# One operation order for every step becomes two tables; weight pairs and expert choice move with it

## The chip, the cores and the metric

The program runs on one core of one Trainium2 chip, in one launch. The metric is device time in microseconds (us) of that core. The engines are TensorE (PE), VectorE (DVE), ScalarE (ACT), GpSimd (POOL) and SyncE (SP, which issues most DMAs here). Each executes its own queue in order, and they wait for each other by semaphores.

## What is computed

Three layers follow each other: attention in which each row keeps its 32 largest scores, a gated dense layer, and a layer in which each token goes to one of eight experts.

```python
def _attn_ref(q, k, v):                     # 4 batches, 8 heads, 576 tokens, 64 wide
    scores = scale * np.matmul(q, k.transpose(0, 1, 3, 2))
    kth = np.partition(scores, -top_k, axis=-1)[..., -top_k:-top_k + 1]
    scores = np.where(scores >= kth, scores, -1000000000.0)
    scores = scores - np.max(scores, axis=-1, keepdims=True)
    attn = np.exp(scores)
    attn = attn / (np.sum(attn, axis=-1, keepdims=True) + 1e-09)
    return np.matmul(attn, v)
def _moe_ref(x, w_in, w_out):               # 2304 tokens, 512 wide, 2048 inside
    h = x @ w_in
    g = h * np.clip(h + 3.0, 0.0, 6.0) / 6.0
    return g @ w_out
def _moe2_ref(x, expert_emb, tau, w1, w2):  # 8 experts, 512 to 1024 to 512
    logits = normalized(x) @ normalized(expert_emb).T / tau
    expert_idx = np.argmax(logits, axis=1)
    ...
        h = np.maximum(x[mask] @ w1[e], 0.0)
        out[mask] = gate_w[mask, None] * (h @ w2[e])
```

The weights `w_in` and `w_out` arrive as 64-bit floats.

## The kernel before

Matrix products are made of parts: an operand x is held as a high part in a format that TensorE takes and a low part x - high, and a product is three matmuls (high·high, high·low, low·high).

**Units and steps.** The attention is cut into 72 units. A unit is 128 query rows of two heads (kind "t"), or the last 64 rows of four heads (kind "r"). The loop has 76 steps. Step i makes the scores of unit i (`scores`, `take`, `pairs`), searches the 32 largest of unit i-1 (`select`, four rounds), masks unit i-2 (`relu`, `mask`), takes the exponent and scales unit i-3 (`expo`, `guard`, `inverse`, `scale`), and turns unit i-4 and multiplies it by V (`turned`, `keep`, `values`, `finish`). Inside this loop nothing is reordered by a scheduler (`tc.manual_schedule`): on each engine the instructions stand as `step` calls them. `scale` runs on ACT for the first 16 units and on POOL afterwards.

**The dense layer** is mixed in. When 256 tokens have their attention, `push_group` queues eight items; one item is taken per step, but not in the eight steps of `PAUSE`. The item's first product `s1` (24 matmuls of 256 columns) fills one PSUM bank, `gate` on ACT and `swish` on DVE read it, `large` on ACT and `small` on POOL make the two parts, and the second product `s2` (12 matmuls of 512 columns) follows a step later. The low parts of the weights lie in DRAM and are fetched again for each group (`fetch`, one item ahead). The first item is taken in step 12; 16 items remain for after the loop.

**The weights** go through 32 pairs of pieces before they can be used. `load_w` issues loads into five staging buffers, `convert_w` turns a pair from 64 to 32 bits (DVE at L221, L223 and, for one piece in four, L229; for the other three ACT at L226 and POOL at L227), and `split_w` makes the high part (ACT) and the low part (POOL, L241) and stores the low part (SP, L236) when it is next called. `words` calls `convert_w` once per step for i < 8 and twice afterwards, so the pairs end in step 19. We call the stretch up to there the ramp.

**Expert choice.** When a group's output leaves PSUM, `route` queues four operations (`r1`, `r2`, `r4`, `r5`) for each of its two blocks of 128 tokens; a step takes one. They make the logits, their argmax (DVE L606 to L609), the token's place in its expert's list (PE, POOL, DVE L619 to L627), and write it to a table in DRAM by an indirect DMA on POOL. After 16 of 18 blocks `order` sorts the experts by load; after the loop a scheduler places the rest of the dense layer, the routing and the expert stage.

The lines that set the order in a step before:

```python
        part(a, 1)                 # s1, then gate, swish
        part(a, 2)
        part(a, 3)
        words()
        for c in range(2):
            at_(4, turned, c)
            at_(4, keep, c)
        at_(0, scores, 0)
```

Of the kernel before, what the change touches and what calls it, by code (L numbers as in the profile page):

```python
# [20 lines left out]
DM, FF = 512, 2048  # L21
# [17 lines left out]
PAUSE = (13, 17, 31, 35, 49, 53, 66, 67)  # L39
HS = S // 2  # L40
# [4 lines left out]
SIDE = 100  # L45
# [38 lines left out]
def layers(tc: tile.TileContext, qt, kt, v, w_in, w_out, embt, tau, w1, w2, out, y_dram, g_dram, x_dram, tbl, lo_dram, flag, pools, consts):  # L84
# [13 lines left out]
    acc = const.tile([128, E], BF16, name="acc")  # L98
# [3 lines left out]
    viol = const.tile([128, NUNIT, 2, 2], BF16, name="viol")  # L102

# [32 lines left out]
    def embed(part):  # L136
# [6 lines left out]
        elif part == 1:  # L143
            onesf = mp.tile([128, 128], F32, tag="ug", name="onesf", bufs=4)
# [15 lines left out]
    def setup():  # L160
        nc.vector.memset(ones, 1.0)
        nc.vector.memset(acc, 0.0)
        nc.gpsimd.iota(iota8, pattern=[[1, 8]], base=0, channel_multiplier=0, allow_small_or_imprecise_dtypes=True)
        nc.gpsimd.iota(ebase, pattern=[[STRIDE, 8]], base=0, channel_multiplier=0, allow_small_or_imprecise_dtypes=True)
# [5 lines left out]
        padt = mp.tile([128, E * STRIDE * 2 // 128], I32, tag="ug", name="padt", bufs=4)  # L170
        nc.gpsimd.memset(padt, PAD)
        nc.sync.dma_start(out=tbl.rearrange("(p a) b -> p (a b)", p=128), in_=padt)
        zr = mp.tile([128, DM], F32, tag="ug", name="zr", bufs=4)
# [7 lines left out]
    wpieces = deque()  # L181
# [7 lines left out]
    wraw = deque()  # L189
    whole_w, small_w = deque(), deque()  # L190
    cnt = [0]

    def load_w():

        while wpieces and len(wraw) < 5:
            src, dst = wpieces.popleft()
            if src.dtype == F32:
# [5 lines left out]
            wraw.append((raw, dst, src.dtype == F32))  # L203

    def convert_w():


        load_w()
        words, two = [], [wraw.popleft() for _ in range(min(2, len(wraw)))]
        if not two:  # L210
            return
        both = mp.tile([128, DM], F32, tag="ug", name="wf", bufs=4)
        for o, (raw, dst, single) in enumerate(two):
            full = both[:, 256 * o:256 * o + 256]
            if single:
                nc.vector.tensor_copy(full, raw)
            else:
                cnt[0] += 1
                words.append((raw, full.bitcast(I32), cnt[0] % 4 != 3))
        for raw, t, _ in words:  # L220
            nc.vector.scalar_tensor_tensor(t, raw[:, :, 1], 3, raw[:, :, 1], op0=ALU.logical_shift_left, op1=ALU.bitwise_xor)  # L221
        for raw, t, _ in words:
            nc.vector.scalar_tensor_tensor(t, t, 0x3FFFFFFF, raw[:, :, 1], op0=ALU.bitwise_and, op1=ALU.bitwise_xor)  # L223
        for raw, t, rounded in words:
            if rounded:
                nc.scalar.activation(raw[:, :, 0], raw[:, :, 0].bitcast(U32), AF.Copy, scale=2.0 ** -29)  # L226
                nc.gpsimd.tensor_tensor(t, t, raw[:, :, 0], op=ALU.add)  # L227
            else:
                nc.vector.scalar_tensor_tensor(t, raw[:, :, 0], 29, t, op0=ALU.logical_shift_right, op1=ALU.bitwise_or)  # L229
        whole_w.append((both,) + two[0][1])  # L230

    def split_w():

        while small_w:
            lo, full = small_w.popleft()
            nc.sync.dma_start(out=lo, in_=full)  # L236
        while whole_w:
            full, hi, lo = whole_w.popleft()
            x = full if len(hi.shape) == 2 else full.rearrange("p (k n) -> p k n", k=2)
            nc.scalar.copy(hi, x)  # L240
            nc.gpsimd.tensor_tensor(x.bitcast(F32R), x, hi.bitcast(F32), op=ALU.subtract)  # L241
            small_w.append((lo, full))
# [4 lines left out]
    def fetch(n, m):  # L247

        if m < total and m not in lows_[n]:
# [224 lines left out]
    def finish(i):  # L474
# [15 lines left out]
        if p == 3:  # L490
            X = xt[b, t // 2]
            if t % 2:
                push_group(X, [4 * b + t - 1, 4 * b + t])

# [595 lines left out]
```

## Time and profile before

| | |
|---|---|
| median of 3 runs | 1183.14 us (1183.0 to 1194.14) |
| the profiled execution, its own time | 1184.85 us |
| its span, first to last instruction | 1183.1 us |
| mean granted TensorE clock | 0.938 |
| busy: PE, DVE, ACT, POOL | 1026.0, 838.1, 732.1, 645.7 us |

The span is the profiled execution without 1.75 us around it. Busy shares are means over stages with different limits, so they are read by stretch. PE's busy time includes modelled ends of matmuls that overlap: a stream of matmuls counts as busy without being at its peak. DVE is the busiest engine in the first fifth, PE from then on.

### The profile page before, as it was taken

The numbers are of one execution on the slowest core, as the hardware profiler recorded it, in microseconds if no ns is written. First come the engines' busy times: TensorE is split into PE (matmuls) and PEld (weight loads), VectorE is DVE, ScalarE is ACT, GpSimd is POOL, SyncE is SP. The second block draws the span as 40 slices with busy tenths as digits, with TensorE's granted clock in tenths as the row PEclk, the third lists the DMA queues.
The fourth block names the chain that finished last, engine by engine and source line by source line (L and its number), as shares of the span: only waits on it lengthen the run. The fifth ranks groups of instructions, "written<-read, shape, count | busy, mean of one in ns | idle before, by whom it ended". The sixth has DMA issues, their size and how long they took to land. (4 is left out here: it accounts for less than half of the span.)

```text
span 1183.1 us, 21477 instructions
## 1 busy us (share of the span) xinstructions
PE 1026.0 (87%) x7224; PEld 885.8 (75%) x7224; DVE 838.1 (71%) x2714; ACT 732.1 (62%) x1518; POOL 645.7 (55%) x846
## 2 busy tenths in 40 slices
PE   2476766699999899999899999999998898999994
PEld 1354555578888788888788878889987787888883
DVE  6999977998899998899998899611244343445440
ACT  5688768777777877777877787642334343444540
POOL 5667767686777786777786766623231433113200
PEclk9966778789999999999999998999998899999997
DMA  7335555655324445424454333346781564244540
GB/s 212 120 100 174 164 177 187 195 179 197 122 90 155 127 160 184 121 89 155 115 183 157 121 92 115 110 142 178 210 276 32 187 217 171 71 176 147 174 166 20
DMA packets 97113, 176.49 MB, mean 149 GB/s; under 512 B 21135, under 2 KB 46882, under 8 KB 96991
## 3 DMA queue, kind: packets, MB, share of 16 engines
q1 hardware_dynamic: 92351, 164.90, 43.4%
q0 software_dynamic: 4640, 10.10, 2.5%
q8 instruction: 60, 0.98, 0.3%
q14 instruction: 62, 0.51, 0.1%
HBM read 155.87 MB, written 19.71 MB: 148 GB/s over the span
## 5 line engine op out<-in xcount | busy, mean ns | idle before, releaser
L420 POOL TENSOR_TENSOR s<-s,z 128x576 f32<-128x576 f32 x144 | 186.0, 1292 | 13.0 <-ACT z L416 11.5
L530 PE MATMUL bank_h<-xh,vh 128*128 128x256 f32 x576 | 172.1, 299 | 2.7 <-ACT xh L488 1.6
L530 PE MATMUL bank_h<-xh,lo 128*128 128x256 f32 x576 | 166.7, 289 | 7.1 <-DMA lo<-lo_dram 7.1
L530 PE MATMUL bank_h<-xl,vh 128*128 128x256 f32 x576 | 166.2, 288 | 0.6 <-DVE xl L489 0.6
L399 DVE MAX8 A<-left 128x8 f32<-128x288 f32 (+1 forms) x288 | 160.0, 596 | 0.0
L453 PE MATMUL bank_t<-ident,s 128*128 128x128 f32 x648 | 110.2, 297 | 53.1 <-ACT s L440 26.1
L547 POOL TENSOR_TENSOR gl<-u,gh 128x512 fp32r<-128x512 f32 x72 | 93.2, 1294 | 79.0 <-ACT gh L544 78.0
L453 PEld LDWEIGHTS bank_t<-ident,s 128*128 128x128 f32 x648 | 76.1, 149 | 75.8 <-ACT pt L458 37.7
L368 PE MATMUL ps_sc<-kst,qh 128*128 128x288 f32 x256 | 88.8, 359 | 49.1 <-ACT s L371 24.1
L536 ACT ACTIVATE u<-bank_h,half 128x512 f32<-128x512 f32 x72 | 49.5, 687 | 118.9 <-PE bank_h L530 118.9
L563 PE MATMUL y<-wh,gh 128*128 128x512 f32 x288 | 120.0, 418 | 0.0
L530 PEld LDWEIGHTS bank_h<-xh,vh 128*128 128x128 f32 x576 | 113.3, 197 | 8.1 <-issue 3.1
L530 PEld LDWEIGHTS bank_h<-xh,lo 128*128 128x128 f32 x576 | 113.2, 196 | 8.3 <-DMA lo<-lo_dram 8.3
L563 PE MATMUL y<-lo,gh 128*128 128x512 f32 x288 | 115.9, 403 | 0.0
L530 PEld LDWEIGHTS bank_h<-xl,vh 128*128 128x128 f32 x576 | 113.4, 197 | 1.4 <-DVE xl L489 1.0
L735 DVE TENSOR_TENSOR l<-a,h 128x1024 fp32r<-128x1024 f32 x64 | 77.4, 1232 | 51.9 <-ACT h L734 45.7
L563 PE MATMUL y<-wh,gl 128*128 128x512 f32 x288 | 114.2, 401 | 0.0
L416 ACT ACTIVATE z<-s,zb 128x576 bf16<-128x576 f32 x144 | 112.7, 782 | 1.0 <-DVE zb L405 0.8
L426 ACT ACTIVATE s<-s,nb 128x576 f32<-128x576 f32 x144 | 111.7, 775 | 0.0
L458 ACT COPY pt<-bank_t 128x384 f32<-128x384 f32 x216 | 95.6, 479 | 24.4 <-PE bank_t L453 24.4
L540 DVE SCALAR_TENSOR_TENSOR u<-u,bank_h 128x512 f32<-128x512 f32 x72 | 49.2, 684 | 83.8 <-ACT u L536 83.7
L471 PE MATMUL bank_a<-pt,vt 128*64 128x128 f32 (+1 forms) x1600 | 105.4, 285 | 0.0
(230 smaller groups left out, 2819.9 us busy)
## 6 DMA issues: line engine op xcount, KB each, us to landing
lo<-lo_dram SPq DMA_DIRECT2D x144, 512.0 KB, 4.3
a<-in_moe_w_dram SPq DMA_DIRECT2D x64, 512.0 KB, 8.7
kraw<-in_k_dram SPq DMA_DIRECT2D x64, 144.0 KB, 2.6
qraw<-in_q_dram SPq DMA_DIRECT2D x64, 128.0 KB, 3.3
w<-in_moe_w_in_dram SPq DMA_DIRECT2D x32, 256.0 KB, 3.9
w<-in_moe_w_out_dram SPq DMA_DIRECT2D x32, 256.0 KB, 3.5
lo_dram<-wf SPq DMA_DIRECT2D x32, 256.0 KB, 2.1
vt<-in_v_dram SPq DMA_DIRECT2D x16, 320.0 KB, 4.1
```

Of the source, the lines that this page charges most:

```text
L368: nc.tensor.matmul(ps[:, n, :HS], t, kk[:, HS * g:HS * g + HS], start=(o == 0), stop=(o == len(parts) - 1))
L399: nc.vector.max(A[:, n, 8 * r:8 * r + 8], src[:, n, :w])
L416: nc.scalar.activation(zb_[n], tile_of(i, n), AF.Relu, bias=sel[i][2][:, n:n + 1], scale=-BIG)
L420: nc.gpsimd.tensor_tensor(s, s, zb_[n], op=ALU.subtract)
L426: nc.scalar.activation(s, s, AF.Exp, bias=sel[i][1][:, n:n + 1], scale=SCALE, accum_out=sums[i][:, n:n + 1])
L453: nc.tensor.transpose(pp[:, 128 * k:128 * k + 128], e[:, 128 * (3 * c + k):128 * (3 * c + k) + 128], ident)
L458: nc.scalar.copy(pts[i][:, 3 * c:3 * c + 3, :].rearrange("p k n -> p (k n)"), tb_.pop((i, c))[:, :384])
L471: nc.tensor.matmul(av[64 * n:64 * n + 64, c0:c1], vt[:, k, 64 * n:64 * n + 64], pt[:, k + 5 * n if k < 4 else 4, c0:c1], start=(o == 0), s ...
L530: nc.tensor.matmul(ph[:, a, :], w, x[:, k, :], start=(k == 0 and n == 0), stop=(k == 3 and n == 2))
L547: nc.gpsimd.tensor_tensor(state[q][1], state.pop((q, "u")).rearrange("p (a n) -> p a n", a=2), state[q][0].bitcast(F32), op=ALU.subtract)
L563: nc.tensor.matmul(state["y"][o], x[:, a, c], w, start=(f == 0 and n == 0), stop=(f == 15 and n == 2))
L735: nc.vector.tensor_tensor(lo, x, hi.bitcast(F32), op=ALU.subtract)
```

## The change

Five things change at once.

- **Two tables.** `step` no longer calls its parts in one written order. Some fifty small operations have names, and a step executes them as the table `FIRST` (i < 21) or `THEN` lists them. `s1` is cut into its two halves (`s10`, `s11`), `finish` into `xh` and `xl`.
- **Weight pairs in fixed phases.** Pair n belongs to step n for n < 5, and from step 5 on each step has two. The loads of a pair stand in the step before it, its conversion (`one`, `two`, `round`, `add`) in its step, high part, low part and store (`hi`, `low`, `store`) in the step after it. The pairs end in step 18.
- **Bounds.** The two DVE instructions per step that make the bias of `relu` (L405) are dropped; the POOL instruction that made the bias of `expo` now makes both, by a table `kb`.
- **Expert choice for four blocks at once.** `choose` and `rank` replace the argmax and the places of four blocks (two outside the loop); `place` writes one block's rows to the DRAM table per step.
- The side work after the loop gets a scheduler priority of 600 in place of 100, and the temporaries live in a pool of three buffers and one of one in place of four.

```diff
+RAMP, WORDS = 5, 21
+FIRST = ("turn0 lows hi0 expo0 low0 hi1 s10 keep0 load_k expo1 turn1 bend0 one0 guard pick0 store0 score0 low1 two0 mask0 pick1 "
+         "turn2 inverse s11 pick2 round1 bend1 keep1 take0 keep2 load_q mask1 s20 score1 round0 gate one1 scale two1 values swish "
...
+THEN = ("pick0 turn0 turn1 expo0 keep0 s10 expo1 lows turn2 pick1 pick2 s11 keep1 keep2 guard bend0 score0 gate take0 load_k "
+        "values mask0 score1 inverse swish scale pick3 bend1 xh load_q take1 prep need_v mask1 bounds aside large s20 xl pairs "
...
-SIDE = 100
+SIDE = 600
...
+    def pair_of(i, c):
+        n = (i if c == 0 else -1) if i < RAMP else 2 * i - RAMP + c
+        return n if 0 <= n < 32 else -1
...
+    def w_one(n):
+        e = ent_[n]
+        e["both"] = mp.tile([128, DM], F32, tag="wf", name="wf", bufs=3)
...
+        for raw, t, _ in words_of(e):
             nc.vector.scalar_tensor_tensor(t, raw[:, :, 1], 3, raw[:, :, 1], op0=ALU.logical_shift_left, op1=ALU.bitwise_xor)
...
+    def w_round(n):
+        for raw, single, rounded in ent_[n]["raws"]:
+            if rounded and not single:
+                nc.scalar.activation(raw[:, :, 0], raw[:, :, 0].bitcast(U32), AF.Copy, scale=2.0 ** -29)
...
+    def w_store(n):
+        e = ent_.pop(n)
+        nc.sync.dma_start(out=e["dst"][1], in_=e["both"])
...
-        else:
-            for n in range(2):
-                nc.vector.tensor_scalar(zb[:, n:n + 1], A[:, n, TOPK - 1:TOPK], BIG, None, op0=ALU.mult)
...
-        nc.gpsimd.tensor_scalar(nb, A[:, :, 0], -SCALE, None, op0=ALU.mult)
+        nc.gpsimd.tensor_tensor(nb, A[:, :, 0:TOPK:TOPK - 1], kb, op=ALU.mult)
...
-            nc.vector.max(mx, l_all[:, g, :])
-            nc.vector.max_index(ix, mx, l_all[:, g, :])
-            nc.vector.tensor_copy(ixf, ix[:, 0:1])
-            nc.vector.tensor_scalar(oh, iota8, ixf, None, op0=ALU.is_equal)
...
+    def choose():
...
+        nc.vector.tensor_reduce(mxs[:, g0:g1], lg, axis=AX.X, op=ALU.max)
+        eq = fs.tile([128, NG, E], F32, tag="df", name="eqs")[:, :n, :]
+        nc.vector.tensor_tensor(eq, lg, wide(mxs[:, g0:g1]), op=ALU.is_equal)
+        nc.vector.tensor_tensor(eq, eq, rev8.unsqueeze(1).broadcast_to([128, n, E]), op=ALU.mult)
...
+    def rank():
...
+        nc.tensor.matmul(pq, tri, picks[:, g0:g1, :].rearrange("p g e -> p (g e)"), start=True, stop=False)
+        nc.tensor.matmul(pq, ones, before[:, g0:g1, :].rearrange("p g e -> p (g e)"), start=False, stop=True)
...
+        nc.vector.tensor_tensor(po, po, picks[:, g0:g1, :], op=ALU.mult)
...
+    def place():
...
+        w_ = nc.gpsimd.indirect_dma_start(out=tbl, out_offset=bass.IndirectOffsetOnAxis(ap=rows[:, g:g + 1], axis=0),
+                                          in_=ids[:, g, :], in_offset=None)
...
+        for name, f, j in (("load", w_load, -1), ("one", w_one, 0), ("two", w_two, 0), ("round", w_round, 0), ("add", w_add, 0),
+                           ("hi", w_hi, 1), ("low", w_low, 1), ("store", w_store, 1)):
+            for c in range(2):
+                ops[name + str(c)] = lambda f=f, j=j, c=c: pair(f, j, c)
+        for name in (FIRST if i < WORDS else THEN).split():
+            ops[name]()
```

**ACT in the ramp**, step 15, the third with an item of the dense layer. L536 is `gate`, L226 the rounding of weight words, L458 `keep`, L371 `take`, L240 the high part of weights. Before:

```order
L488 CAST xh<-bank_a 128x128
L416 ACTIVATE z_151<-s_144,zb 128x576
L426 ACTIVATE s_143,sums<-s_143,nb 128x576
L536 ACTIVATE u<-bank_h,half 128x512
L226 ACTIVATE w_1674<-w_1674 128x256
L226 ACTIVATE w_1708<-w_1708 128x256
L458 COPY pt<-bank_t_120 128x384
L458 COPY pt<-bank_t_121 128x384
L458 COPY pt<-bank_t_120 128x384
L371 COPY s_146<-ps_sc 128x2x288
L226 ACTIVATE w_1824<-w_1824 128x256
```

The same step now, where L575 is `gate`, L246 the rounding, L483 `keep`, L399 `take`, L441 `relu` and L259 the high part:

```order
L451 ACTIVATE s_148,sums<-s_148,nb 128x576
L441 ACTIVATE z_156<-s_149,nb 128x576
L246 ACTIVATE w_1768<-w_1768 128x256
L246 ACTIVATE w_1770<-w_1770 128x256
L441 ACTIVATE z_157<-s_149,nb 128x576
L483 COPY pt<-bank_t_126 128x384
L399 COPY s_151<-ps_sc 128x2x288
L483 COPY pt<-bank_t_125 128x384
L246 ACTIVATE w_1763<-w_1763 128x256
L575 ACTIVATE u<-bank_h,half 128x512
L465 ACTIVATE s_148<-s_148,sums 128x576 x2
```

`gate` stood third in the step and ahead of every `keep` and `take`; it now stands behind them and behind all three roundings.

**SP in the ramp**, step 16 before (L236 stores a low part, L288 loads K, L251 fetches low parts for the dense layer, L202 loads weight words):

```order
L236 DMA lo_dram_62<-wf 128x512 x2
L288 DMA kraw<-in_k_dram 128x288 x4
L251 DMA lo_1987<-lo_dram_61 128x1024
L202 DMA w_1992<-in_moe_w_in_dram 128x512
L202 DMA w_1994<-in_moe_w_out_dram 128x512
L202 DMA w_2028<-in_moe_w_out_dram 128x512
L202 DMA w_2030<-in_moe_w_out_dram 128x512
L251 DMA lo_2073<-lo_dram_62 128x1024
```

One step of the ramp now (L267 stores, L279 fetches, L347 loads Q, L218 loads weight words, those of the next step):

```order
L267 DMA lo_dram_61<-wf 128x512
L279 DMA lo_1707<-lo_dram_61 128x1024
L347 DMA qraw<-in_q_dram 128x2x128
L267 DMA lo_dram_62<-wf 128x512
L218 DMA w_1761<-in_moe_w_in_dram 128x512
L218 DMA w_1763<-in_moe_w_in_dram 128x512
L218 DMA w_1768<-in_moe_w_out_dram 128x512
L218 DMA w_1770<-in_moe_w_out_dram 128x512
```

The loads stood between the fetches of their own step, behind both stores; they now stand last, for the step to come.

**DVE in the loop**, one block of 128 tokens before, with the copy of its logits (L601) and its argmax (L606 to L609) between `pairs` (L384) and `select` (L399):

```order
L384 TENSOR_TENSOR left<-ps_sc,left 128x2x144
L601 COPY l_all<-bank_t_121 128x8
L606 MAX mx<-l_all 128x8
L607 MAX_INDEX ix<-mx,l_all 128x8
L608 CAST ixf<-ix 128x1
L609 TENSOR_SCALAR oh<-iota_81,ixf 128x8
L352 TENSOR_TENSOR kst<-kraw,kst 64x288 x2
L399 MAX A<-top 128x8 x2
```

The first `choose` now, between the last round of `select` (L427) and `pairs` (L408):

```order
L427 MAX A<-left 128x8 x2
L659 TENSOR_REDUCE mxs<-l_all 128x4
L661 TENSOR_TENSOR eqs<-l_all,mxs 128x32
L662 TENSOR_TENSOR eqs<-eqs,rev_89 128x32
L664 TENSOR_REDUCE first<-eqs 128x4
L665 TENSOR_TENSOR picks<-eqs,first 128x32
L408 TENSOR_TENSOR ps_sc<-ps_sc,s_150 128x2x144
```

What stood there for each block of 128 tokens stands there once for four.

## Rows read from the trace of the kernel before

**Rows 1.** The page, 40 slices of the span: DVE busy tenths, granted TensorE clock.

```profile
DVE  6999977998899998899998899611244343445440
...
PEclk9966778789999999999999998999998899999997
```

**Rows 2.** Windows: length, busy PE, PEld, DVE, ACT, POOL, granted clock, DMA share, GB/s.

```profile
15.00:126.00 111.00, 64.77 (x334) 49.62 (x335) 110.39 (x382) 83.93 (x182) 75.63 (x100) 0.75 0.46 145
126.00:256.00 130.00, 90.54 (x605) 76.62 (x604) 110.36 (x354) 95.08 (x208) 90.56 (x111) 0.80 0.55 177
256.00:749.00 493.00, 472.63 (x3835) 410.54 (x3833) 454.45 (x1649) 376.09 (x831) 355.85 (x500) 0.99 0.43 137
749.00:900.00 151.00, 145.77 (x1026) 130.37 (x1025) 42.08 (x131) 58.60 (x112) 48.44 (x53) 1.00 0.58 178
900.00:1183.00 283.00, 249.32 (x1424) 216.72 (x1422) 116.81 (x191) 110.57 (x173) 67.33 (x68) 0.95 0.40 139
```

**Rows 3.** Line L380, first of `pairs`: duration min/median/max, first and last start.

```profile
L380 DVE TENSOR_TENSOR ps_sc<-ps_sc,s x72: 443/451/467, 14.6 to 748.9; 128x288 f32<-128x288 f32 x72
```

**Rows 4.** Waits, 126 to 256 us: in total, times, longest.

```profile
ACT w L226 <- DMA w<-in_moe_w_in_dram: 12.1, 3, 5.4
DVE u L540 <- ACT u L536: 9.7, 3, 5.5
ACT w L226 <- DMA w<-in_moe_w_out_dram: 9.4, 3, 4.0
ACT u L536 <- PE bank_h L530: 8.8, 2, 6.1
```

**Rows 5.** Waits of SP's own queue, 126 to 256 us.

```profile
SPq L236 <- POOL wf L241: 48.9, 16, 8.2
SPq L202 <- POOL wf L227: 21.0, 14, 7.0
```

**Rows 6.** Timeline of ACT, 164 to 182 us: start, duration, idle before in brackets.

```profile
174.60 0.69 ACT L536 ACTIVATE u<-bank_h,half 128x512 f32<-128x512 f32 x1 [6.06 <-PE bank_h L530]
```

**Rows 7.** Timeline of PE, 164 to 182 us, inside one `s1`.

```profile
170.27 0.42 PE L530 MATMUL bank_h<-xh,lo 128*128 128x256 f32 x1
170.48 0.42 PE L530 MATMUL bank_h<-xh,vh 128*128 128x256 f32 x1
...
173.74 0.28 PE L530 MATMUL bank_h<-xl,vh 128*128 128x256 f32 x1
173.86 0.28 PE L530 MATMUL bank_h<-xh,lo 128*128 128x256 f32 x1
```

**Rows 8.** Groups by line of DVE, 15 to 256 us: busy, mean ns, idle before.

```profile
L221 DVE SCALAR_TENSOR_TENSOR wf<-w 128x256 int32<-128x256 int32 x62 | 29.0, 502 | 4.1 <-DMA w<-in_moe_w_in_dram 3.4 <-DMA w<-in_moe_w_out_dram 0.7
L223 DVE SCALAR_TENSOR_TENSOR wf<-wf,w 128x256 int32<-128x256 int32 x62 | 23.9, 425 | 0.0
L229 DVE SCALAR_TENSOR_TENSOR wf<-w,wf 128x256 int32<-128x256 int32 x16 | 6.6, 416 | 0.0
```

**Rows 9.** Groups by line of DVE, 256 to 749 us.

```profile
L405 DVE TENSOR_SCALAR zb<-A 128x1 f32<-128x1 f32 x102 | 13.8, 144 | 0.0
L626 DVE SCALAR_TENSOR_TENSOR po<-po,oh 128x8 f32<-128x8 f32 x11 | 10.2, 927 | 0.0
L609 DVE TENSOR_SCALAR oh<-iota,ixf 128x8 bf16<-128x8 f32 x11 | 7.3, 665 | 0.4
L606 DVE MAX8 mx<-l_all 128x8 f32<-128x8 f32 x11 | 1.9, 170 | 0.4
...
L626 DVE DVE_READ_ACCUMULATOR po<-po,oh 128x1 f32 x11 | 0.8, 77 | 0.0
```

**Rows 10.** Line L626: duration ns min/median/max, first and last start.

```profile
L626 DVE SCALAR_TENSOR_TENSOR po<-po,oh x18: 157/647/1147, 307.0 to 909.7; 128x8 f32<-128x8 f32 x18
```

**Rows 11.** Window of 18 steps in the loop, columns as in rows 2.

```profile
450.60:624.70 174.10, 165.83 (x1358) 143.87 (x1358) 161.68 (x585) 134.28 (x299) 127.67 (x177) 1.00 0.45 139
```

**Rows 12.** DMA issues: count, KB each, median us to landing.

```profile
w<-in_moe_w_in_dram SPq DMA_DIRECT2D x32, 256.0 KB, 3.9
```

More of the change, by code (lines that the diff above doesn't have):

```diff
@@ L202, in load_w @@
                 nc.sync.dma_start(out=raw, in_=src.bitcast(I32).rearrange("p (n two) -> p n two", two=2))
[L203 to L214, printed above, removed]
-            if single:
-                nc.vector.tensor_copy(full, raw)
-            else:
-                cnt[0] += 1
-                words.append((raw, full.bitcast(I32), cnt[0] % 4 != 3))
-        for raw, t, _ in words:
+                cnt[0] += 1
@@ L230, in convert_w, with parts_of @@
[L230 to L242, printed above, removed]
+    def parts_of(e):
+        hi, full = e["dst"][0], e["both"]
+        return hi, full if len(hi.shape) == 2 else full.rearrange("p (k n) -> p k n", k=2)
@@ L648, in whole, with part @@
         return item
-    def part(item, k):
+    def part(item, k, *half):
         if item:
-            item[k](item[0])
+            item[k](item[0], *half)
     late = {}
@@ L776, in step @@
     def step(i, last):
+        a = moe.popleft() if moe and i not in PAUSE else None
         def at_(j, f, *a):
@@ L779, in at_ @@
                 f(i - j, *a)
-        more = iter(range(1 if i < 8 else 2))
-        def words():
-            if next(more, None) is not None:
-                convert_w()
-        a = moe.popleft() if moe and i not in PAUSE else None
-        at_(2, relu, 0)
-        at_(2, mask, 0)
-        at_(3, expo, 0)
-        lows()
-        split_w()
-        load_k(i + 2)
-        at_(1, select, 0)
-        at_(1, select, 1)
-        part(a, 1)
-        part(a, 2)
-        part(a, 3)
-        words()
@@ L800, in step @@
-        for c in range(2):
-            at_(4, turned, c)
-            at_(4, keep, c)
-        at_(0, scores, 0)
-        at_(4, turned, 2)
-        at_(4, keep, 2)
-        at_(0, take, 0)
-        at_(1, select, 2)
-        words()
-        at_(3, expo, 1)
-        at_(3, guard)
-        if last:
-            last[6](last[0], 0)
-        part(a, 4)
-        part(a, 5)
-        at_(0, scores, 1)
-        at_(0, take, 1)
-        at_(1, select, 3)
-        at_(3, inverse)
-        if i - 3 >= EARLY:
-            at_(3, scale)
@@ L878, in layers @@
                         side.popleft()()
+                with tc.high_priority(offset=SIDE):
+                    if chosen[0] < scored[0] and scored[0] % 2 == 0:
+                        choose()
+                        rank()
+                    while spots:
+                        place()
             last = whole(moe.popleft() if moe else None, last)
```

233 lines of the change are left out of this document (142 added, 91 removed).

## The prediction

> **What bounds the kernel now.** I read the slices first. DVE stands at 9 for the first third of the ramp, while the granted clock swings between 6 and 9; later DVE drops and the clock holds at 9 [rows 1]. Line L380 opens `pairs`, once per unit; its 72 starts run from 14.6 to 748.9 us, so a step takes 734.3/71 = 10.3 us on average [rows 3]. The windows then cut the span [rows 2]:
>
> - 15 to 126 us: DVE is busy 110.4 of 111.0 us. DVE is the bound, nothing else.
> - 126 to 256 us, the second half of the ramp: no engine is full. DVE has 110.4 of 130.0 us, ACT 95.1, PE and POOL 90.5; 19.6 us of DVE are idle.
> - 256 to 749 us, the loop: PE 472.6 of 493.0, DVE 454.5. PE leads, DVE is close behind.
> - 749 to 900 and 900 to 1183 us: PE 145.8 of 151.0 and 249.3 of 283.0.
>
> The waits of 126 to 256 us tell why nobody is full [rows 4]. ACT waits 12.1 + 9.4 = 21.5 us at L226 for weight words that have not landed, and 8.8 us in `gate` for `s1`; `swish` on DVE waits 9.7 us for `gate`. One `gate` blocked ACT for 6.06 us [rows 6], with every `keep` and `take` of that step behind it. The loads come late because SP, in order, waits 48.9 us before stores for POOL's low part and 21.0 us before loads for a free staging buffer [rows 5].
>
> **The change part by part.** The sum is made against the span, 1183.1 us.
>
> *Pairs moved earlier.* A pair costs DVE (29.0 + 23.9 + 6.6)/31 = 1.92 us [rows 8]. Steps 5, 6 and 7 now have two pairs and not one, so the first stretch gets 3 × 1.92 = 5.8 us more and the second stretch 5.8 us less.
>
> *Bounds.* Two DVE instructions of 0.144 us leave each step [rows 9]: 0.29 × 11 steps = 3.2 us in the first stretch, 2.6 us in nine steps of the second, 13.8 us in the loop. In exchange `relu` now waits for POOL's `bounds`, which stands one step ahead of it; POOL is busy 355.9 of 493.0 us in the loop [rows 2], and this slack hides it. Without that cover, ACT would wait up to about one POOL instruction per step, with `gate` and `take` behind it.
>
> *First stretch.* DVE is the bound there, so its work counts in full: + 5.8 - 3.2 = **+ 2.6 us**.
>
> *Second stretch.* DVE's work falls to 110.4 - 5.8 - 2.6 = 102.0 us. That is the floor. The new order takes both causes of the idle time away in part. Loads are issued a step ahead, so `round` on ACT meets words that have had most of a step to land, against 3.9 us from issue to landing [rows 12]. And `gate` stands behind all `keep` and the rounding, so when `s1` is late, ACT and DVE have other work: on DVE three of four rounds of `select` and both conversions come ahead of `swish`. What stays is the clock (below), the embedding's norm with its two table loads, and that ACT's 95.1 us must still alternate with DVE. Floor 102, ceiling 130; I let half of the 19.6 us of idle time stay, since the two waits named first, 21.5 us on ACT and 9.7 us on DVE, are not the only ones: 102.0 + 9.8 = 111.8 us, so **- 18.2 us**.
>
> *Loop: choice.* Per block of 128 tokens, before: L626 0.927, L609 0.665, and seven more of 0.077 to 0.170 us that sum to 0.96, so 2.55 us, or 10.2 us for four blocks [rows 9]. Now nine instructions serve four blocks. The trace of before does not have them. Their bounds: nine of the shortest, 9 × 0.17 = 1.5 us, and, if every one of four that read two tiles in SBUF is stretched as L626 was at its worst, 4 × 1.147 + 5 × 0.17 = 5.4 us [rows 9, 10]. I take the upper one, as L626 in the loop is nearer to its worst than to its best: 4.8 us saved per four blocks, three times in the loop.
> The rows show one instruction, L626, at anything from 0.157 to 1.147 us [rows 10], so something else stretches it. The Trainium skill says in "SBUF — State Buffer", section "SBUF: two separate sides", that a DVE instruction with two SBUF inputs and a GpSimd instruction that reads SBUF exclude each other for a whole instruction. By that rule the upper price, 5.4 us, would be the usual one wherever POOL is at work, and the part saves 4.8 us per four blocks; without it the lower price, 1.5 us, and 8.7 us. The trace agrees with the rule as far as L626 goes; no row here shows the new instructions.
>
> *Loop: order.* DVE loses 13.8 + 3 × 4.8 = 28.2 us of 454.5 there. But PE's work is the same, but for a few matmuls of 8 columns, so the most that the loop can give is PE's idle time, 493.0 - 472.6 = 20.4 us. Over 18 steps, one period of units, PE idles 174.1 - 165.8 = 8.3 us and DVE 12.4 [rows 11]. Two of 18 steps have no new item, and there PE has to wait for DVE whatever the order. In the others the new order puts `scores` and `take` well ahead of `pairs`, and `s2`, which waits for nothing in its step, last. I take a third of PE's idle time: 20.4/3 = **- 6.8 us**. What is late next there is PE itself. That `s1` is cut in two has no row that prices it alone; I take nothing for it, and at most one distance between starts, 0.21 us per item [rows 7].
>
> *After the loop.* PE is busy 145.8 of 151.0 us to 900 us, so choice, `place` and priority 600 lie beside it. At about 900 us the last two blocks' places hold the experts; `choose` for both together ends when the second has its logits, where before the first was placed sooner but the second decided. I take **0**, with 5 us either way, out of the 33.7 us in which PE idles there [rows 2].
>
> Sum: 2.6 - 18.2 - 6.8 + 0 = - 22.4 us. The span becomes 1160.7, the profiled execution 1162.4, which is 1.7 us over the median of before; on the median's scale, 1183.1 - 22.4 = **1160.7 us**.
>
> **The rivals.**
>
> *All waits go* (1140 us). The second stretch reaches its floor, - 28.0, the loop gives two thirds of PE's idle time, - 13.6, the end gives 4: 2.6 - 28.0 - 13.6 - 4 = - 43. For it: the waits named are far larger than the idle time. Against it: ACT, at 95.1 of 130 us, would be at 93% in 102 us.
>
> *The clock keeps the ramp long* (1174 us). In one `s1` of the ramp matmuls started 0.21 us apart, later in it 0.12, as the clock rose from one level (1.2 GHz) to the other (2.4 GHz) [rows 7], so its 24 matmuls take 5.0 or 2.9 us. PE was busy 90.5 us in the second stretch at a granted clock of 0.80 [rows 2], some 72 us at full clock. If the clock fell to 0.6 there, PE would need 121 us and be the bound: + 2.6 - 9 - 3 = - 9. For it: the ramp's clock already follows PE's gaps. Against it: a shorter step leaves smaller gaps. Here the change does what it says and little comes of it.
>
> *The loads become DVE's first wait* (1200 us, slower). `one0`, the first work on DVE in a ramp step, now needs words whose load stands last on SP, behind `store1` and behind buffers that only POOL's `add` frees. SP's 48.9 and 21.0 us of such waits [rows 5] are not removed, they are moved. If `add` comes late in the step, a load lands 3.9 us later [rows 12], and DVE stands still with all of `select` and `pairs` behind. It decides where a load is issued less than 3.9 us before the step ends. I price it at 3 us, most of one landing, in each of the 13 steps with two pairs: the first stretch has seven of them, 7 × 3 + 2.6 = + 23.6 us; the second has six, 111.8 + 18 = 129.8, so - 0.2. With the loop's - 6.8 that makes + 16.6, some 1200 us. Against it: a `swish`, a round of `select` and the five instructions of `pairs` follow the last conversion on DVE, time in which a load can land; and the buffers of one pair of the two come free earlier than the other's.
>
> **How the numbers follow.** The forecast (1150 to 1170) has 0.45, all waits gone 0.20, the clock 0.20, the late loads 0.15. The likeliest time is 1160 us. The range leaves out the lower half of the second case and the upper half of the last: **1139 to 1188 us**. One per cent, some 12 us, is what a measurement of this kernel can tell from no change. Faster by over 1% means under 1171.3: 0.43 of the forecast, 0.20, and 0.04 of the clock, 0.67. Slower means over 1195: half of the last case and mishaps of the same sign that I did not name, 0.13. Within 1%: 0.20.
>
> **What the changed profile would show.** The step starts of `pairs`: the 72nd start should come near 748.9 - 22.4 = 726.5 us [rows 3], and DVE should be full to about 129 us. Waits for weight words on ACT should fall from 21.5 us to a few, and `gate`'s wait for `s1` stay without a wait on DVE behind it. In the loop DVE's busy time should fall by 20 to 30 us and PE's share of the stretch rise above 0.96. The end from the loop's last unit to the last instruction should stay within 5 us of 1183.1 - 748.9 = 434.2. I am wrong if L380's starts in the ramp are not closer together, if DVE's first conversion waits for a DMA, or if the loop's 18 steps stay at 174 us.

## The result and the profile after

The changed kernel takes 1171.43 us (median of four runs, 1169.73 to 1173.43) against 1183.07 of the kernel before, a ratio of 0.9879 with a 95% interval of 0.9839 to 0.992. It is faster, by 12 us in the medians and some 14 by the ratio, where 22 were forecast. The time lies in the range by luck: the sum came out so by terms that missed in opposite directions.

In the slices of the page (40 of 29.2 us), DVE now stands at 9 through the ramp, behind the first slice (two of its slices stood at 7 before, [rows 1]); the granted clock is still 5 to 7 tenths in the third to the seventh slice:

```profile
DVE  6999999999788999888988789811243344444440
...
PEclk9966577899999999999989999999999899999998
```

The line that opens `pairs` is L408 now, with 72 starts as L380 in [rows 3]:

```profile
L408 DVE TENSOR_TENSOR ps_sc<-ps_sc,s x72: 436/456/467, 13.1 to 745.1; 128x288 f32<-128x288 f32 x72
```

By these starts the span falls into four stretches, cut at the 12th, 21st and 72nd unit in both kernels:

| stretch, by the starts of `pairs` | before | after | change | forecast |
|---|---|---|---|---|
| ramp, to the 12th unit | 126.4 us | 145.1 us | + 18.7 | + 2.6 |
| ramp, 12th to 21st unit | 129.9 | 118.4 | - 11.5 | - 18.2 |
| loop, 21st to 72nd unit | 492.6 | 481.6 | - 11.0 | - 6.8 |
| 72nd unit to the end | 434.2 | 422.8 | - 11.4 | 0 |
| span | 1183.1 | 1167.9 | - 15.2 | - 22.4 |

The ramp as a whole, to the 21st unit, is 7.2 us longer, where 15.6 us less were forecast; the loop and the end gave 22.4 us where 6.8 were forecast. From the first to the 12th start, without what comes before the first, it is 111.8 us before and 132.0 after.

The windows of the kernel after show the same stretches (columns as in [rows 2], whose rows they answer to):

```profile
13.10:145.10 132.00, 66.92 (x341) 53.32 (x341) 131.50 (x377) 89.15 (x195) 90.28 (x110) 0.73 0.45 145
145.10:263.50 118.40, 85.95 (x620) 76.11 (x621) 116.18 (x321) 90.31 (x196) 89.31 (x108) 0.83 0.58 181
263.50:745.10 481.60, 461.87 (x3821) 415.26 (x3819) 429.65 (x1472) 381.85 (x833) 348.50 (x496) 0.99 0.45 139
745.10:890.00 144.90, 140.47 (x966) 126.48 (x965) 43.18 (x99) 55.58 (x104) 49.16 (x54) 0.99 0.63 186
890.00:1167.90 277.90, 249.50 (x1452) 218.07 (x1450) 116.73 (x187) 111.87 (x176) 68.09 (x68) 0.96 0.41 141
```

The second row is the surprise. The idle time of DVE did go: 116.18 of 118.4 us are busy, where 110.36 of 130.0 were. But DVE's work did not fall to 102 us, it rose. Over the whole ramp, cut at the 21st unit, DVE was busy 221.13 of 241.7 us before and 247.68 of 250.4 after: 17.9 us of idle time are gone and 26.5 us of work have come, though DVE has fewer instructions (697 against 736).

The waits of 145 to 263 us show that what the prediction wanted to remove is removed. DVE waits for nothing but a sum:

```profile
DVE sums L458 <- POOL sums L455: 1.6, 2, 0.9
```

ACT waits no more for weight words, and `gate` holds it less (3.6 us in three times; [rows 4] had 21.5 and 8.8):

```profile
ACT s L465 <- DVE sums L458: 11.0, 4, 3.8
ACT gh L583 <- DVE u L579: 5.4, 6, 1.5
ACT pt L483 <- PE bank_t L478: 4.3, 2, 4.1
ACT u L575 <- PE bank_h L567: 3.6, 3, 1.6
```

SP's own waits in the same stretch, which were 48.9 and 21.0 us [rows 5]:

```profile
SPq L267 <- POOL wf L263: 21.4, 10, 4.3
SPq L218 <- POOL wf L251: 12.9, 8, 3.5
SPq L218 <- DVE A L427: 9.9, 4, 2.5
```

The loads (L218) wait no less than before, 22.8 us by these two lines, but for words of the step to come.

Where the work has come from, the groups of DVE by line from 13 to 264 us say. L234, L238 and L241 are the same three instructions as L221, L223 and L229 in [rows 8]:

```profile
L238 DVE SCALAR_TENSOR_TENSOR wf<-wf,w 128x256 int32<-128x256 int32 x63 | 40.8, 686 | 0.0
L234 DVE SCALAR_TENSOR_TENSOR wf<-w 128x256 int32<-128x256 int32 x62 | 33.8, 584 | 0.1
L241 DVE SCALAR_TENSOR_TENSOR wf<-w,wf 128x256 int32<-128x256 int32 x16 | 17.5, 1091 | 0.0
```

The conversions took 29.0 + 23.9 + 6.6 = 59.5 us before and take 33.8 + 40.8 + 17.5 = 92.1 us now: + 32.6 us for the same instructions (141 of them in the window against 140). Less the 20 × 0.29 = 5.8 us of the dropped bias, that leaves 26.8, about the 26.5 us. To the 12th unit they take 51.5 us against 28.9, from there to the 21st 40.7 against 30.4, with three pairs less. One step shows it. DVE and POOL, timeline of the step from 119.8 us, start and duration first; first DVE:

```profile
122.25 0.75 DVE L234 SCALAR_TENSOR_TENSOR wf<-w 128x256 int32<-128x256 int32 x2
...
123.89 1.95 DVE L238 SCALAR_TENSOR_TENSOR wf<-wf,w 128x256 int32<-128x256 int32 x2
125.77 1.49 DVE L241 SCALAR_TENSOR_TENSOR wf<-w,wf 128x256 int32<-128x256 int32 x1
...
130.47 0.74 DVE L238 SCALAR_TENSOR_TENSOR wf<-wf,w 128x256 int32<-128x256 int32 x2
```

and POOL, where L445 is `mask`:

```profile
124.10 2.88 POOL L445 TENSOR_TENSOR s<-s,z 128x576 f32<-128x576 f32 x2
126.94 0.92 POOL L251 TENSOR_TENSOR wf<-wf,w 128x256 int32<-128x256 int32 x1
```

The pair of L238 at 130.47 us, with POOL idle, takes 0.74 us. The pair at 123.89 us meets the first mask and takes 1.95, and L241, issued just after the second mask begins, ends 0.3 us after that mask. So these DVE instructions, which read two tiles in SBUF, seem to stand still until POOL's instruction is over; conv_late and mask_out test that. The step is 12.7 us long where the like step of the kernel before had 11.4.

### The profile page after: what moved, and what is told of

Read it like the earlier page. It is cut to its first block, busy times and chain, and to the rows that moved or that the text cites. A ratio compares the mean times of both kernels' runs of the same rounds, so it can differ in the third digit from the quotient of the medians.

```text
span 1167.9 us, 21262 instructions
## 1 busy us (share of the span) xinstructions
PE 1007.7 (86%) x7200; PEld 891.2 (76%) x7200; DVE 841.2 (72%) x2461; ACT 736.1 (63%) x1518; POOL 651.7 (56%) x849
## 5 line engine op out<-in xcount | busy, mean ns | idle before, releaser
L445 POOL TENSOR_TENSOR s<-s,z 128x576 f32<-128x576 f32 x144 | 190.1, 1325 | 62.6 <-ACT z L441 61.3
L567 PE MATMUL bank_h<-xh,vh 128*128 128x256 f32 x576 | 177.2, 308 | 0.8 <-DVE u L579 0.8
L427 DVE MAX8 A<-left 128x8 f32<-128x288 f32 (+1 forms) x288 | 159.7, 595 | 0.0
L586 POOL TENSOR_TENSOR gl<-u,gh 128x512 fp32r<-128x512 f32 x72 | 93.0, 1292 | 84.7 <-ACT gh L583 72.2
L483 ACT COPY pt<-bank_t 128x384 f32<-128x384 f32 x216 | 100.7, 475 | 58.6 <-PE bank_t L478 58.2
L396 PEld LDWEIGHTS ps_sc<-kst,qh 128*128 128x128 f32 x256 | 54.7, 214 | 92.5 <-issue 70.7
L478 PEld LDWEIGHTS bank_t<-ident,s 128*128 128x128 f32 x648 | 83.4, 152 | 46.0 <-ACT s L465 14.4
L602 PE MATMUL y<-wh,gh 128*128 128x512 f32 x288 | 116.1, 404 | 0.0
L399 ACT COPY s<-ps_sc 128x576 f32<-128x576 f32 x144 | 91.4, 635 | 38.5 <-PE ps_sc L396 34.9
L441 ACT ACTIVATE z<-s,nb 128x576 bf16<-128x576 f32 x144 | 111.6, 779 | 3.7 <-POOL nb L435 3.7
```

Source lines behind the costliest of these rows:

```text
L396: nc.tensor.matmul(ps[:, n, :HS], t, kk[:, HS * g:HS * g + HS], start=(o == 0), stop=(o == len(parts) - 1))
L399: nc.scalar.copy(sbuf[i % NS][:, :, HS * g:HS * g + HS], ps_[i][:, :, :HS])
L427: nc.vector.max(A[:, n, 8 * r:8 * r + 8], src[:, n, :w])
L441: nc.scalar.activation(zb_[n], tile_of(i, n), AF.Relu, bias=sel[i][1][:, n, 1:2], scale=-BIG)
L445: nc.gpsimd.tensor_tensor(s, s, zb_[n], op=ALU.subtract)
L478: nc.tensor.transpose(pp[:, 128 * k:128 * k + 128], e[:, 128 * (3 * c + k):128 * (3 * c + k) + 128], ident)
```

## The experiments

Each comparison had its own runs of the kernel before, whose medians went from 1183 to 1199 us; so kernels of different comparisons are set side by side by their ratios, and by places in their profiles. In kernels whose tables are written on one line, line numbers are two less (L236 is L238, L239 is L241, L406 is L408), as far as no other edit shifts them.

**conv_late: the conversions behind both masks.**

```diff
-FIRST = "... bend0 one0 guard pick0 store0 score0 low1 two0 mask0 pick1 ... round0 gate one1 scale two1 values ..."
+FIRST = "... bend0 guard pick0 store0 score0 low1 mask0 pick1 ... round0 gate one0 one1 two0 two1 scale values ..."
```

> The changed kernel with one table edit: in the ramp the conversions (one, two) of both pairs stand together behind both masks, where POOL has little left to do; nothing else moves. Theory (a DVE conversion with two SBUF tiles waits out POOL's mask): L238 falls from 0.71 to about 0.41 us, L241 from 1.49 to 0.41, a ramp step before the dense layer from 12.7 to 11.2-11.5 us, and the time to 1150-1158 us. Rival (the conversions are slow for a reason of their own, such as ACT's rounding on the same tile or the DMA traffic): they stay as long, the step stays at 12.7, the time stays at 1168-1174 us.

Measured: 1151.21 us, ratio 0.9699 (0.9668 to 0.973). Groups of DVE, 13 to 246 us:

```profile
L232 DVE SCALAR_TENSOR_TENSOR wf<-w 128x256 int32<-128x256 int32 x62 | 35.5, 626 | 0.0
L236 DVE SCALAR_TENSOR_TENSOR wf<-wf,w 128x256 int32<-128x256 int32 x63 | 26.3, 455 | 0.0
L239 DVE SCALAR_TENSOR_TENSOR wf<-w,wf 128x256 int32<-128x256 int32 x16 | 6.6, 411 | 0.0
```

The conversions take 68.4 us, 23.7 less than in the changed kernel (59.5 in the kernel before; L236 came to 0.46 us, not to 0.41, and L232 is no shorter than L234 was: in the step from 119.8 us its four begin beside the second mask). A two-pair step before the dense layer takes 10.8 to 11.9 us, and the 21st unit starts at 245.4 us, 18.1 earlier. One table edit that moves nothing but four names is worth more than the whole change was (ratio 0.9879 to 0.9699). The theory holds for L236 and L239; this is the best version of the study (conv_embed, below, equals it).

**mask_out: the suspected cause taken away.**

```diff
     def mask(i, n):
+        if i < 17:
+            return
```

> The changed kernel with POOL's mask left out for the first 17 units (their rows are not masked); tables and everything else stay, relu on ACT too. Theory (a DVE conversion waits out a POOL instruction on SBUF): with nothing else moved L241 falls from 1.49 to about 0.41 us and L238 from 0.71 to 0.42-0.55, and a ramp step before the dense layer from 12.7 to 11.2-11.6 us, as in conv_late. Rival (the place among ACT's roundings or the DMAs stretches them): L241 stays above 1 us, the step at 12.3 or more.

Only its ramp is read here: what follows works on other values, and the whole, 1250.46 us once, is not compared. Groups of DVE, first the changed kernel, 107.1 to 145.1 us (three steps before the dense layer):

```profile
L238 DVE SCALAR_TENSOR_TENSOR wf<-wf,w 128x256 int32<-128x256 int32 x12 | 8.1, 712 | 0.0
L241 DVE SCALAR_TENSOR_TENSOR wf<-w,wf 128x256 int32<-128x256 int32 x3 | 4.5, 1492 | 0.0
L234 DVE SCALAR_TENSOR_TENSOR wf<-w 128x256 int32<-128x256 int32 x12 | 4.5, 412 | 0.0
```

then mask_out, 107 to 145 us (its 12th unit starts at 126.5):

```profile
L234 DVE SCALAR_TENSOR_TENSOR wf<-w 128x256 int32<-128x256 int32 x14 | 5.8, 456 | 0.0
L238 DVE SCALAR_TENSOR_TENSOR wf<-wf,w 128x256 int32<-128x256 int32 x14 | 5.7, 444 | 0.0
L241 DVE SCALAR_TENSOR_TENSOR wf<-w,wf 128x256 int32<-128x256 int32 x4 | 1.6, 412 | 0.0
```

With every instruction of DVE, ACT and SP where it was, L241 falls from 1.49 to 0.41 us, L238 from 0.71 to 0.44, and a ramp step before the dense layer from 12.7 to 10.5 us, further than expected. L241 and L238 give about 1.1 us a step each, which is the whole; L234 has no part in it there (0.41 us in these steps with the mask and without). The rounding on ACT and the DMAs are still there, so they did not stretch L238 and L241; POOL's mask did.

**ramp_old and ramp_loads: the ramp in the order before.**

```diff
-FIRST = "turn0 lows hi0 expo0 low0 hi1 s10 keep0 ..."
+FIRST = "bend0 mask0 expo0 lows hi0 low0 store0 load_k pick0 pick1 s10 s11 gate swish one0 two0 round0 add0 turn0 keep0 turn1 keep1
+         score0 turn2 keep2 take0 pick2 one1 two1 round1 add1 expo1 guard s20 large small score1 take1 pick3 inverse bend1 mask1
+         bounds s21 hi1 low1 store1 pairs load0 load1 load_q prep scale values xh xl need_v aside"
```

> The changed kernel with the ramp's table in the order of the kernel before (conversions, gate, swish and keep where they stood), loads a step ahead and the new phases kept. Theory (the new order lengthened the first stretch by collisions and shortened the second by taking waits away): a two-pair step before the dense layer falls from 12.7 to about 11.4 us, DVE's idle time in the steps with dense items returns (10 us or more), the time is 1165-1177 us. Rival (the phases themselves, three more pairs early and the loads a step ahead, made the first stretch longer): the steps stay at 12.7 and the time rises to 1180 us or more.

Measured: 1203.25 us, ratio 1.0122 (1.0084 to 1.016). Neither side was right, though the time is on the rival's. The first two-pair steps take 12.5 us, those behind them up to the dense layer 14 to 18, though the conversions are short again (L236 0.42, L239 0.42 us). The waits of DVE, 80 to 200 us, say why:

```profile
DVE wf L232 <- DMA w<-in_moe_w_in_dram: 14.4, 7, 4.3
DVE wf L232 <- DMA w<-in_moe_w_out_dram: 6.7, 6, 2.2
```

This is the prediction's third rival, in an order that the change did not choose: the loads stand last in a step and the conversions early in the next. The second kernel moves the loads alone:

```diff
-... round0 add0 turn0 ... round1 add1 expo1 ... pairs load0 load1 load_q ...
+... round0 add0 load0 turn0 ... round1 add1 load1 expo1 ... pairs load_q ...
```

> As ramp_old (the ramp in the order of the kernel before), but each pair's loads are issued right behind its predecessor's add and not at the step's end. Theory (in ramp_old the early conversions met loads issued last in the step, which cost DVE 30% of its time): steps 8 to 11 fall from 14-18 us to 11.4-12.5, DVE is busy over 0.95 of them, and the 20th step comes 15-30 us sooner than in ramp_old (289.3 us). Rival (another wait of the old order, relu behind bounds, holds the steps): they stay above 13.5 us.

Measured: 1176.18 us once, beside 1195.53 of the kernel before. DVE's waits for words all but vanish, steps 8 to 10 take 12.2 us and step 11 14.1, with DVE busy 0.93 to 0.94 and 0.81 of them, and the 21st unit starts at 265.7 us, 23.6 sooner. Step 11 and DVE's share fall a little short of what was expected, but the loads were the cause. What the ramp now holds longest in that stretch is another wait:

```profile
ACT s L463 <- DVE sums L456: 21.4, 9, 4.3
```

**loop_old and loop_old_zb: the loop in the order before, without and with the bias on DVE.**

```diff
-THEN = "pick0 turn0 turn1 expo0 keep0 s10 ..."
+THEN = "bend0 mask0 expo0 lows load_k pick0 pick1 s10 s11 gate swish turn0 keep0 turn1 keep1 score0 turn2 keep2 take0 pick2 expo1
+        guard s20 large small score1 take1 pick3 inverse scale bend1 mask1 bounds s21 pairs load_q prep values xh xl need_v aside place"
```

> The changed kernel with the loop's table (from step 21) in the order of the kernel before; bounds, choice and the ramp stay new. Theory (the loop's 11 us come from the order, since PE leads there): all of it goes, the loop from step 20 to 71 takes 490-493 us and the time is 1179-1184 us. Rival (they come from the 25 us of DVE work that is gone): the loop stays within 3 us of 481.6 and the time at 1168-1174 us.

Measured: 1210.68 us, ratio 1.0177 (1.0135 to 1.0219). The loop from the 21st to the 72nd unit takes 520.6 us, not 490 to 493: 39 more than after, and 28 more than in the kernel before. Not only the order's gain went. ACT's longest wait, 300 to 760 us:

```profile
ACT z L439 <- POOL nb L433: 62.0, 42, 3.9
```

`relu`, first in a step of the old order, stands there behind POOL's `bounds`. So the bias goes back to DVE, on top of the old order:

```diff
+        else:
+            for n in range(2):
+                nc.vector.tensor_scalar(sel[i][2][:, n:n + 1], A[:, n, TOPK - 1:TOPK], BIG, None, op0=ALU.mult)
...
-        nc.scalar.activation(zb_[n], tile_of(i, n), AF.Relu, bias=sel[i][1][:, n, 1:2], scale=-BIG)
+        nc.scalar.activation(zb_[n], tile_of(i, n), AF.Relu, bias=sel[i][2][:, n:n + 1], scale=-BIG)
```

> As loop_old (the loop's table in the order of the kernel before), but relu's bias is made on DVE again by two instructions of 0.144 us at the end of select, as in the kernel before. Theory (in the old order relu stands right behind POOL's bounds, and the wait for it stretched the loop to 520.6 us): ACT's waits for nb at relu, 62.0 us between 300 and 760 us in loop_old, vanish, and the loop from step 20 to 71 takes 489-496 us as in the kernel before. Rival (something else of the change, the choice or the places, does not bear the old order): it stays above 510 us.

Measured: ratio 1.0027 (0.9996 to 1.0059). The window of its loop:

```profile
266.90:762.60 495.70, 470.76 (x3810) 409.15 (x3810) 436.35 (x1573) 375.07 (x830) 346.85 (x495) 0.99 0.44 135
```

495.7 us, as the kernel before (492.6), with new choice, new places and all. Two instructions of 0.144 us on DVE were worth 24.9 us there.

**zb_back: the bias on DVE, the new tables.** The same edit on the changed kernel.

> The changed kernel, new tables, with relu's bias made on DVE again (two instructions of 0.144 us per step). Theory (DVE's work counts only where DVE is full): the 20th step comes 4-6 us later, the loop from step 20 to 71 takes 481-484 us as without them, the time is 4-7 us over the changed kernel's. Rival (the loop's gain is DVE work that is gone): the loop takes 488-495 us and the time is 12-20 us over it.

Measured: ratio 0.9924 (0.9895 to 0.9953), so some 5 us over the changed kernel by the ratios, whose intervals overlap. The 21st unit starts 3.4 us later (266.9), a little less than expected, and the loop is not longer:

```profile
266.90:747.80 480.90, 460.76 (x3823) 414.07 (x3822) 438.08 (x1574) 381.93 (x833) 348.04 (x496) 0.99 0.46 139
```

So in the new order dropping the bias gives the loop nothing; against loop_old_zb, which differs by the table alone, the new order gives 495.7 - 480.9 = 14.8 us, one profile each (the ten other profiles with this loop table, mask_out among them, have 479.0 to 485.9 us). ACT's waits show what the table moves. First the kernel before, 300 to 740 us:

```profile
ACT u L536 <- PE bank_h L530: 62.2, 40, 4.7
ACT pt L458 <- PE bank_t L453: 13.8, 46, 0.9
```

then the changed kernel, the same window:

```profile
ACT pt L483 <- PE bank_t L478: 42.9, 63, 2.1
ACT s L399 <- PE ps_sc L396: 24.4, 49, 1.8
ACT u L575 <- PE bank_h L567: 9.7, 32, 0.9
```

loop_old_zb has 60.2 us of the first in 35 times. `gate` hardly waits for `s1` any more, but `keep` and `take` wait for PE themselves; ACT's waits for everything fall from 103 to 92 us only. That the table makes the loop shorter is shown; by which of these waits is not.

**choice_each: choice per block in the loop.**

```diff
-        if g % 4 == 3 and g < 12:
+        if g < 12:
             side.extend((choose, rank))
```

> The changed kernel with choose and rank called in the loop for each block of 128 tokens, and not for four at once; after the loop as it was. Theory (PE leads in the loop, so 9 to 13 us of DVE work more are hidden): the loop from step 20 to 71 stays within 2 us of 481.6, the time within 3 us of the changed kernel's. Rival (choice for four at once is worth a good part of the loop's 11 us): the loop takes 486-492 us.

Measured: 1170.73 us, ratio 0.9813 (0.978 to 0.9845). The loop (264.6 to 743.6 us) takes 479.0 us, with DVE busy 15.2 us more than in the changed kernel (444.82 against 429.65). Choice for four blocks at once saves DVE time, and none of it shows in the loop.

**side100, tail_each, both_back: after the loop.**

```diff
-SIDE = 600
+SIDE = 100
```

> The changed kernel with the priority of the side work after the loop back at 100. Theory (600 made the stretch after the loop 11 us shorter, by having the choice and the sorting of the experts earlier): from the last unit's pairs to the end it takes 432-436 us again and the time is 1179-1184 us. Rival (the choice for two blocks together, or the pools of temporaries, did it): it stays at 421-425 us, the time at 1168-1174 us.

```diff
-                    if chosen[0] < scored[0] and scored[0] % 2 == 0:
+                    if chosen[0] < scored[0]:
```

> The changed kernel with choose and rank called after the loop for each block, and not for two at once; the loop as it was. Theory (the rest of the gain after the loop, some 9 us behind the last dense item, comes from the last blocks' rank standing behind matmuls of the first expert on PE, not from doing two at once): within 2 us of the changed kernel. Rival (two at once make the end shorter): 4-9 us longer from the last dense item's first matmul to the end, 293 us in the changed kernel.

Measured: side100 1174.3 us, ratio 0.9891 (0.9861 to 0.9921), 425.6 us from the 72nd unit to the end; tail_each 1175.26 us, ratio 0.9849 (0.9815 to 0.9882), 301.0 us from the last dense item to the end. Of the first the theory falls: the priority is not it. The second is at the rival's end, but the profiles don't bear the rival out: from the last dense item to the end, zb_back takes 299.5 us, ramp_old 300.3, choice_each 295.4 and conv_late 291.6, and after the loop these four are written as the changed kernel (293.2). A difference of 8 us there is no effect of an edit. The waits differ in the expert stage: PE waits for gathered tokens (L816) 8 to 16 us in all, up to 7.6 us at a time, and at other places in other profiles.

One thing is the same in all. In the kernel before PE waits once for the last block's one-hot:

```profile
PE bank_t L615 <- DVE oh L609: 4.4, 1, 4.4
```

and in none of the others. The 97th matmul of the first expert starts 50.7 us behind the last dense item before, 46.1 after, 47.7 in side100 and 46.7 in tail_each. The last run undoes both edits at once.

> The changed kernel with both edits after the loop undone at once: priority 100, and choose and rank for each block. The kernel before had one wait of 4.4 us on PE for the last block's one-hot, 28 us behind the last dense item; neither side100 nor tail_each alone has one there. Theory (the two edits together removed it, each covers for the other): a wait of 3-5 us for picks is back on PE. Rival (the new functions themselves stand elsewhere in the queue, whatever the priority): none there, and the stretch from the last dense item to the 97th matmul of the first expert stays at 46-49 us, against 50.7 in the kernel before.

Measured: 1177.71 us once, beside 1199.33, with 300.1 us from the last dense item to the end. No wait for picks is there, and the 97th matmul comes at 47.3 us. PE's longest waits behind 760 us:

```profile
PE pxt L816 <- DMA xg<-y_dram,idt: 12.0, 4, 6.5
PE bank_t L816 <- DMA xg<-y_dram,idt: 3.8, 1, 3.8
```

So the rival holds: neither priority nor the pairing removed the wait, the new functions stand behind the first expert's matmuls on PE in any case. Of the 9.0 us behind the last dense item (302.2 to 293.2), the 4.6 us up to the 97th matmul are the change's (1.8 to 4.8 in the versions of this study, with 48.9 to 45.9 us); what makes up the rest isn't settled. In all profiles of the new functions the stretch from the 72nd unit takes 420.9 to 431.1 us, against 434.2 in the one profile of the kernel before.

**conv_embed: an attempt to take the next wait.** In conv_late PE waits 6.9 us for DVE's squares of the embedding, with the next `s1` behind it. (The edit also moves `onesf` to another buffer, not shown here.)

```diff
-            emb["pe"] = pe = half_a()
-            for k in range(4):
-                nc.tensor.matmul(pe[:, :E], onesf, sq[:, k, :], start=(k == 0), stop=(k == 3))
+            emb["in"] = onesf, sq
         elif part == 2:
+            onesf, sq = emb["in"]
+            emb["pe"] = pe = half_a()
+            for k in range(4):
+                nc.tensor.matmul(pe[:, :E], onesf, sq[:, k, :], start=(k == 0), stop=(k == 3))
```

> As conv_late, and the embedding's eight matmuls stand a step later, so that PE does not wait for DVE's squares with the next s1 behind them (6.9 us in step 15). If that wait holds steps 15 and 16 (17.0 and 16.5 us, DVE busy 0.86 and 0.82), they fall to 13-15 us each and the time is 3-6 us under conv_late's. If the dense layer's first steps are held by gate and swish between ACT and DVE, they stay at 16-17 us and the time stays.

Measured: 1151.9 us, ratio 0.9635 (0.9583 to 0.9687), which overlaps with conv_late's. Step 15 fell from 17.0 to 12.7 us and step 16 rose from 16.5 to 18.4. The wait went along with the matmuls, 150 to 215 us:

```profile
PE bank_a L163 <- DVE xl L523: 5.5, 1, 5.5
```

It is named for `xl` now, which reads from the bank that the matmuls write to. The last dense item starts at 856.1 us against 854.3, so the two are equal within what this study can tell; the squares alone were not the cause.

## Why the prediction came out as it did

- **Second stretch: the mechanism was right, its floor was wrong.** The waits named there went as forecast: words from 21.5 us to none on ACT, `gate` from 8.8 to 3.6, DVE's idle time from 19.6 to 2.2 us. But the floor of 102 us took DVE's durations over from the rows of before, and DVE needed 116.2: the step that failed in the first stretch failed here too.
- **First stretch: the step that failed.** "Its work counts in full: + 5.8 - 3.2" was priced with the conversions' means in the old order, 0.425 us for L223 and 0.416 for L229. In the new order these instructions lie beside POOL's mask and take 0.69 and 1.09 us on the mean; all the ramp's conversions together cost 32.6 us more, which is more than the 17.9 us of idle time that the table removed. In this stretch they cost + 22.6 us where + 5.8 was forecast, in the second + 10.3 where - 5.8 was. conv_late and mask_out show the cause from both sides. The rows of before held a sign of it: L221 took 0.502 us on the mean [rows 8], and a pair of it 1.55 us beside a mask at 108 us, against 0.74 in the same step. The prediction had the rule before it and used it on other instructions alone: the Trainium skill says in "SBUF — State Buffer", section "SBUF: two separate sides", that a DVE instruction with two SBUF inputs and a GpSimd instruction that reads SBUF exclude each other for a whole instruction. I weighed it for three calls of `choose`, worth a few us, and not for the conversions that the same table moved. The trace agrees with it: 0.41 us alone, 1.49 us beside a mask of 1.44.
- **Loop: right sign, mis-sized, and the wrong source.** - 6.8 was a third of PE's idle time; it was - 11.0 by the starts of `pairs`. PE's idle time did not shrink (20.4 to 19.7 us); its busy time did, 472.2 to 461.9, for as many matmuls (3832 and 3821 in the records), so the busy time that I took as a floor was none; what it holds besides work, no run here separates. The gain is the table's: 14.8 us by itself (zb_back against loop_old_zb). The 28.2 us of DVE work counted beside it (24.7 measured) were worth nothing in the loop, as zb_back and choice_each show. One sign named for being wrong came true as well: the 18 steps of [rows 11], from the 41st to the 59th unit, take 174.4 us after, and 174.0 before. The 11.0 us come from the 33 other steps; one of the 18 takes 12.8 us, with PE waiting 3.6 for POOL's `scale`, and in conv_late the 18 take 171.0.
- **Bounds: no wait in the new order, as forecast, but not for the reason given.** The cover was named as POOL's slack; it is rather the place of `relu` in the new table, well behind `bounds`: POOL has more slack in loop_old (347.8 of 520.6 us busy), and ACT waits there. In the old place the wait cost 24.9 us in the loop.
- **After the loop: 0 (± 5) was too little by 11.4 us**, of which 9.0 lie behind the last dense item. One wait of 4.4 us on PE went, in every version of the new functions; profiles with the same text after the loop differ by 8 us there, so the rest can't be assigned, and that it came to 11.4 is in part luck.
- **Rivals.** "All waits go" came true for the ramp's waits and did not give its time, for the reason above. The clock did not decide: it was granted 0.78 over the ramp before and after. The late loads did not come: DVE's only wait in the second stretch is 1.6 us for a sum. ramp_old shows that the mechanism is real, with 21 us of such waits in 120, where the conversions stand early; in the new tables they stand late enough.
- **The other signs.** "I am wrong if L380's starts in the ramp are not closer together": up to the 12th unit they are further apart (12.0 us a step against 10.2), behind it closer (13.2 against 14.4). The 72nd start came at 745.1 us and not near 726.5, and PE's share of the loop stayed at 0.96.

The change as given is worth 14 us; with its conversions out of POOL's way it is worth 36 (3.0%).

## What to carry to other kernels

A duration read from a trace belongs to the neighbours that it had there: before an order is changed, look which DVE instructions with two tiles in SBUF come to lie beside POOL's long ones, and price them at up to what is left of POOL's instruction plus their own time (1.21 + 0.41 us for L241 in the step above, which took 1.49). An instruction that looks like pure cost may be the cover of a wait (two of 0.144 us were worth 24.9 us in one order and nothing in another), so drop it together with the move that makes it needless, and look at both. Where an engine is full, idle time that a new order removes from it is only a gain if the order does not give the engine more to do.

## What the runs showed of the hardware that was not expected

- DVE instructions that read a single tile seem to be stretched beside POOL too. In the changed kernel's loop L681, a conversion of four numbers per partition from one tile to integers, takes 1.27 us on the mean of two; L659, a reduction of 32 numbers from one tile, takes 0.17:

```profile
L681 DVE CAST rows<-de 128x4 int32<-128x4 f32 x2 | 2.5, 1273 | 0.1
...
L659 DVE TENSOR_REDUCE mxs<-l_all 128x4 f32<-128x32 f32 x3 | 0.5, 170 | 0.0
```

  Both times POOL's `small` (L586, 1.30 and 1.27 us) begins 0.04 to 0.05 us before L681 and ends with it. After the loop, with two numbers per partition and no POOL instruction beside it, L681 takes 0.17 us three times. L659 ran beside POOL's `scale` (L467) and was not stretched. What POOL did beside L681 was not varied by an edit, so that it is the same exclusion is argued from these five.
- The conversion L234, which reads one tile twice, is stretched as well: 0.41 us in the steps before the dense layer, 0.70 on the mean between the 12th and the 21st unit, 0.54 there in mask_out.
- POOL's own instruction can be longer beside such a DVE instruction: the two masks beside conversions took 2.88 us together, and 2.52 in conv_late, where `select` and only one conversion lie beside them; over the ramp a mask takes 1.42 us on the mean, 1.31 in conv_late and 1.29 in the kernel before.
